# A new order of all engines from 45 microseconds on, in an attention and maxout kernel on one core

## The chip, the core and the metric

The kernel runs on one core of a Trainium2 chip. The metric is the time of one execution on the device, in microseconds, as the median of several runs. The engines of the core are TensorE (PE in the profile; its weight loads are PEld), VectorE (DVE), ScalarE (ACT), GpSimd (POOL) and SyncE (SP), which here issues nearly all transfers.

## What is computed

Attention over queries that are averaged in pairs, 8 batches of 8 heads with 1152 keys and 64 values each, and behind it a layer with two hidden projections of which the larger is taken:

```python
q_pool = q.reshape(B, H, S // 2, 2, D).mean(axis=3)        # B, H, S, D = 8, 8, 1152, 64
scores = scale * np.matmul(q_pool, k.transpose(0, 1, 3, 2))
attn = np.exp(scores - scores.max(-1)); attn = attn / attn.sum(-1)
x = np.matmul(attn, v)                                     # to (8 * 576, 512)
g = np.maximum(x @ w1, x @ w2)                             # w1, w2: 512 x 1024
return g @ w_out                                           # w_out: 1024 x 512
```

The kernel uses that max(a, b) = max(a − b, 0) + b: with wd = w1 − w2 and w21 = w2 w_out, the result is relu(x wd) w_out + x w21.

## The kernel before

Two heads that stand side by side are a *pair*; there are 32 pairs, four to a batch. For each pair SyncE loads q, k and v (576 KB each, lines 346, 358, 370) into rings of three buffers. GpSimd casts them to bfloat16: k at L405, v at L445, and q at L435, where the two rows of a query are also added. k is turned by a DMA transpose from SyncE (L475, `kT`), q on VectorE by eight 32 x 32 block transposes (L485, `qpT`), from pair 5 on.

The scores of all pairs are one stream of 324 *groups* of 512 columns (`scores`, L302). The two heads of a pair use the upper and lower 64 rows of the array at once, so a group is two rows' worth of matmuls with 64 contraction rows. One exp on ScalarE (L317) empties a group from two banks of PSUM into `et`. Attention (`av_jobs`) multiplies the exps by v with 128 contraction rows (L621), and the leftover 64 queries of a pair by blocks of 64 columns (L636). VectorE takes the reciprocal of the sums and multiplies (L651, L654) into `xnat`. The result is turned by a DMA transpose (L703, `xT`) or on TensorE (L552, L730, evacuated at L733, L738).

The second layer has *hidden-layer jobs* (h, L760), which make relu(x wd) for two blocks of 128 features over up to 512 tokens, and *projection jobs* (p, L803), which make 256 rows of the result. Both use 64-row halves: a first half-job runs every contraction block with the halves one way round, a second half-job the other way round into the same two banks. At the second half-job's start the plan puts a fence, a wait of TensorE for the end of the first:

```python
                    return ([f"wd{ct}.{half}" for half in range(2)] + xkeys(ct, n0, n1),
                            0.2135 * size / 512 + 0.0025, "s", turn == 1 and ct == 0, go)
```

h jobs are evacuated at L771 (VectorE) or L775 (ScalarE), p jobs at L809 or L812. At the end three jobs for the last 256 rows use the whole array (L846).

No scheduler runs on the chip. The order is written out by hand as tables that a search made: `LOADS` is the order of the loads on SyncE, `MOE` the order of the h, p and w jobs, `BANKS` the PSUM bank of each job and score group, and a long string of letters (L957 on) the order of all steps, one letter each. `S` is a group of scores, `E` its exp, `A` a block of attention, `a` its evacuation, `l` the next load, `r` one of the eight transposes of q, `t` a DMA transpose of k, `x` one of a result, and the digits 0 to 3 are one unit of the h or p job open in that slot, 4 to 7 its evacuation on VectorE, `8`, `9`, `+` and `-` the same on ScalarE. Each engine executes its own steps in the order of the string, and waits by semaphores for what a step reads or overwrites. From group 40 on a load also waits for the exp two groups back (`pace`):

```python
        def pace():
            g = done[0] - PACE
            return [f"E{g}"] if PACE and g >= PACE_FROM else []
```

Of the kernel before, what the change touches and what calls it, by code (L numbers as in the profile page):

```python
# [116 lines left out]
def bass_funnel_attn__then__act_maxout2_kernel(  # L117
# [39 lines left out]
    W_DIFFS = ((3, 0), (3, 1), (1, 0), (2, 0), (2, 1), (0, 0), (0, 1), (1, 1))  # L157
# [24 lines left out]
    )  # L182
    MOE = (
        "wwhhhhpphhhhpphhhhhhhhpphhhhpphhhhphhhhpphhhhphhhhphhhhpphhhhhhhhhphphh"
    )
    BANKS = (
        "0124605424023623462032424660232342630240624702402064202420472042646264246024604640164604264126402406"
        "0240260240246304260346204040640606062061262062062402740264062402406402640642704260202402402406401640"
        "6460462056204620462046042164206204620620426026402602602602604604614646046046024604604204620420642040"
        "6406406742064264264206520640260462620620162062046206240620206204230642042042424126426046046045620642"  # L190
        "6024062046206206206206412640246056046206404024024026423236042642042626260262626426454526420642064206"
        "2454"
# [849 lines left out]
```

## Time and profile before

| | us |
|---|---|
| median of 3 runs | 358.24 |
| the runs | 357.92, 358.24, 360.69 |
| the profiled execution's own time | 358.12 |
| its span, first to last instruction | 356.4 |
| TensorE busy | 346.0 |
| ScalarE busy | 313.8 |
| VectorE busy | 230.1 |
| GpSimd busy | 151.4 |

The time of an execution is 1.7 us longer than its span. In the profile a line such as "L760 PE MATMUL ps<-xT,wd" names the source line, the engine, the operation and what it writes and reads. A matmul's duration includes its way through the array, so the pace of matmuls is read from their starts. TensorE's clock was granted in full: 0.999 of it over the span.

### The profile page before, as it was taken

To read this page: it belongs to the slowest core of one execution; us is meant where nothing else is said; L and a number is where in the kernel's file an instruction comes from. 1 tells how busy PE (TensorE), PEld (TensorE's weight loads), DVE (VectorE), ACT (ScalarE), POOL (GpSimd) and SP (SyncE) were. 2 spreads that over 40 slices of the span, in tenths; PEclk is the share of its full clock that TensorE was granted. 3 is DMA by queue.
4 is the path that set the end of the run, shared out by engine and by line. 5 is a ranking of instruction groups with operands and counts; after the bars stand their busy time and mean duration, and the time that the engine had idled before them with its cause. 6 is when DMAs were issued, how large, how long until landed. Compare 5 with 4: busy or idle time off the path is not lost.

```text
span 356.4 us, 13757 instructions
## 1 busy us (share of the span) xinstructions
PE 346.0 (97%) x6178; PEld 218.5 (61%) x6178; DVE 230.1 (65%) x472; ACT 313.8 (88%) x354; POOL 151.4 (42%) x136
## 2 busy tenths in 40 slices
PE   7889999999899999999999999999999999999996
PEld 5556665656564675656666576556576757448753
DVE  2587589974966867985887677785586875414001
ACT  5999999999999899999999989989999796992431
POOL 2625997554564264355544455227444621010000
PEclk9999999999999999999999999999999999999999
DMA  8999999999989989998999699998999943012215
GB/s 271 403 397 398 370 255 309 280 289 261 293 252 279 315 196 350 237 301 183 278 320 260 153 230 301 237 314 234 224 299 255 267 68 75 17 32 47 61 31 148
DMA packets 76699, 84.55 MB, mean 237 GB/s; under 512 B 48480, under 2 KB 49760, under 8 KB 76640
## 3 DMA queue, kind: packets, MB, share of 16 engines
q1 hardware_dynamic: 75856, 83.15, 87.5%
q8 instruction: 48, 0.79, 0.9%
q10 hardware_dynamic: 784, 0.52, 0.5%
q14 instruction: 11, 0.09, 0.1%
HBM read 62.91 MB, written 9.44 MB: 203 GB/s over the span
## 4 chain that ended last, share of the span: by engine, by line
PE 87%; ACT 9%; DMA 2%; issue 1%; SPq 0%; DVE 0%
PE ps L803 25%; PE ps L621 20%; PE ps L302 19%; PE ps L760 16%; ACT et L317 9%; PE ps L636 3%; PE ps L593 2%; DMA qraw<-in_q_dram 2%; PE ps L846 1%; PE ps L552 0%; PE ps L533 0%; SPq L346 0%; DVE qp L428 0%; SPq L358 0%; PE ps L730 0%
## 5 line engine op out<-in xcount | busy, mean ns | idle before, releaser
L317 ACT ACTIVATE et<-ps 128x1024 bf16<-128x1024 f32 (+1 forms) x336 | 302.4, 1019 | 14.5 <-PE ps L302 9.7
L302 PE MATMUL ps<-qpT,kT 64*128 64x256 bf16 (+7 forms) x1162 | 117.3, 283 | 2.7 <-issue 1.1
L485 DVE STREAM_TRANSPOSE qpT<-qp 32x288 bf16<-32x288 bf16 x216 | 101.4, 469 | 10.4 <-PE ps L302 6.1
L760 PE MATMUL ps<-xT,wd 64*128 64x512 bf16 (+3 forms) x832 | 81.2, 311 | 0.2
L302 PEld LDWEIGHTS ps<-qpT,kT 64*128 64x128 bf16 x1162 | 48.3, 94 | 49.7 <-ACT et L317 11.3
L803 PE MATMUL ps<-wo,stage 64*128 64x512 bf16 x544 | 76.4, 376 | 0.0
L435 POOL TENSOR_TENSOR qp<-qraw 128x576 bf16<-128x576 f32 x30 | 42.1, 1406 | 61.1 <-DMA qraw<-in_q_dram 57.3
L621 PEld LDWEIGHTS ps<-vE,et 128*128 128x128 bf16 x1728 | 54.9, 97 | 13.9 <-ACT et L317 9.3
L621 PE MATMUL ps<-vE,et 128*128 128x65 bf16 x1728 | 60.7, 193 | 0.7 <-issue 0.3
L771 DVE TENSOR_SCALAR stage<-ps 128x1024 bf16<-128x1024 f32 (+3 forms) x41 | 39.7, 970 | 21.1 <-PE ps L760 20.6
L760 PEld LDWEIGHTS ps<-xT,wd 64*128 64x128 bf16 x832 | 35.6, 94 | 22.2 <-PE ps L760 1.9
L405 POOL TENSOR_SCALAR kbf<-kraw 128x1152 bf16<-128x1152 f32 x31 | 35.7, 1153 | 26.3 <-DMA kraw<-in_k_dram 25.6
L803 PE MATMUL ps<-w,xT 64*128 64x512 bf16 x272 | 40.8, 377 | 0.0
L803 PEld LDWEIGHTS ps<-wo,stage 64*128 64x128 bf16 x544 | 26.4, 94 | 20.5
L445 POOL TENSOR_SCALAR vE<-vraw 128x1152 bf16<-128x1152 f32 x24 | 27.4, 1154 | 19.4 <-PE ps L636 10.8
L809 DVE COPY stage<-ps 128x1024 f32<-128x1024 f32 x14 | 17.1, 1224 | 23.1 <-PE ps L803 23.0
L468 POOL TENSOR_SCALAR stage<-et 128x1152 bf16<-128x1152 bf16 x14 | 16.1, 1152 | 35.5 <-ACT et L317 35.5
L654 DVE TENSOR_TENSOR xnat<-ps,rc 128x256 bf16<-128x256 f32 (+2 forms) x71 | 27.6, 397 | 2.0
L651 DVE RECIPROCAL rc<-ps 128x4 f32<-128x4 f32 (+2 forms) x64 | 11.6, 182 | 25.9 <-PE ps L621 25.5
L621 PEld LDWEIGHTS ps<-stage,et 128*128 128x128 bf16 x576 | 18.1, 97 | 2.7 <-issue 2.6
L621 PE MATMUL ps<-stage,et 128*128 128x65 bf16 x576 | 19.7, 193 | 0.0
L803 PEld LDWEIGHTS ps<-w,xT 64*128 64x128 bf16 x272 | 12.5, 94 | 8.8 <-DVE stage L771 0.2
(55 smaller groups left out, 155.4 us busy)
## 6 DMA issues: line engine op xcount, KB each, us to landing
vraw<-in_v_dram SPq DMA_DIRECT2D x32, 576.0 KB, 6.1
kraw<-in_k_dram SPq DMA_DIRECT2D x31, 576.0 KB, 6.7
qraw<-in_q_dram SPq DMA_DIRECT2D x31, 576.0 KB, 6.3
out_dram<-stage SPq DMA_DIRECT2D x24, 256.0 KB, 4.1
out_dram<-stage SPq DMA_DIRECT2D x21, 128.0 KB, 3.4
xT<-in_moe_w_dram SPq DMA_DIRECT2D x4, 512.0 KB, 12.2
stage<-in_moe_w_out_dram SPq DMA_DIRECT2D x4, 512.0 KB, 14.1
stage<-in_moe_w_dram SPq DMA_DIRECT2D x4, 512.0 KB, 13.2
```

The source lines that it names most:

```text
L302: last = e.matmul(ps[:, h, col:col + hi - lo], kT[i % 3][rows(h), t, :], qpT[i % 3][rows(h), lo:hi], start=True, stop=True)
L317: op("ACT", lambda e: e.activation(et2[:, :, c:c + z - a], ps[:, :, a - g * W:z - g * W], EXP, scale=scale), r=[f"b{m}", f"b{m + 1}"], w=w ...
L405: op("POOL", lambda g: g.tensor_scalar(kbf[s][:, :, :, :].rearrange("p t h d -> p h t d"), kraw[r][:, :, :, :], 1.0, 1.0, ALU.mult, ALU.mu ...
L435: op("POOL", lambda g: g.tensor_tensor(qpf[s][:, :, :], qraw[r][:, :, 0, :], qraw[r][:, :, 1, :], ALU.add), r=[f"qraw{r}"], w=[f"qp{s}.0", ...
L445: return g.tensor_scalar(vE[r][:, :, :, 0:D].rearrange("p t h d -> p h t d"), vraw[s][:, :, :, :], 1.0, 1.0, ALU.mult, ALU.mult)
L485: op("DVE", lambda e: e.transpose(view[dst:dst + 32, :, 32 * pb:32 * pb + 32], qpf[s][src:src + 32, :, 32 * db:32 * db + 32]), r=[f"qp{s}. ...
L621: last = e.matmul(fb[m][:, at * 66:at * 66 + 65], et[:, a:a + P], vE[vs][:, t, half, 0:65], start=(t == 0), stop=(t == NT - 1))
L654: todo.append(evac_op("DVE", lambda e, m, z=z, at=at, num=num, dst=dst: e.tensor_tensor(dst, a(m)[z, at:at + num, 0:D], rc[k][z, at:at + n ...
L760: last = e.matmul(fb[m + k][:, 0:size], wd[z, ct, (f0 + k) * P:(f0 + k + 1) * P], xT[z, ct, n0:n1], start=(turn == 0 and ct == 0), stop=(t ...
L771: return e.tensor_scalar_max(gT[:, f0:f0 + 2, g0:g0 + size], wide[m // 2][:, :, 0:size], 0.0)
L803: last = e.matmul(fb[m + k][:, :], lhs, rhs, start=(turn == 0 and j == 0), stop=(turn == 1 and j == NC_ + NF - 1))
L809: return e.tensor_copy(osb2[:, o:o + 2, :], wide[m // 2][:, :, :])
```

## The change

Only the tables change: one place of `W_DIFFS` (two of the subtractions w1 − w2 swapped), the tail of `LOADS`, one line of `MOE`, `BANKS`, and the string of steps. Up to about 45 us each engine's order is as before. The h and p jobs now rotate through the four slots 0 to 3, where before they used two, and up to four are open at a time. The numbers and shapes of all instructions stay, but for the evacuations: 10 on ScalarE where it was 14 (without the last one, L854), and four more on VectorE. The diff, cut:

```diff
-    W_DIFFS = ((3, 0), (3, 1), (1, 0), (2, 0), (2, 1), (0, 0), (0, 1), (1, 1))
+    W_DIFFS = ((3, 0), (3, 1), (1, 0), (2, 0), (0, 0), (2, 1), (0, 1), (1, 1))
...
-        ("v", 12), ("q", 13), ("v", 13), ("k", 15), ("q", 14), ("v", 14), ("k", 16), ("v", 15),
...
+        ("q", 13), ("q", 14), ("k", 15), ("k", 16), ("v", 12), ("v", 13), ("v", 14), ("q", 15),
...
-        "wwhhhhpphhhhpphhhhhhhhpphhhhpphhhhphhhhpphhhhphhhhphhhhpphhhhhhhhhphhh"
+        "wwhhhhpphhhhpphhhhhhhhpphhhhpphhhphhhhhpphhhhphhhhphhhhpphhhhhhhphhhhp"
...
-        "6024062046206206206206412640246056046206404024024026423236042642042626260262626426454526420642064206"
-        "2454"
+        "6024063046216206206216402640240656046026404024024026431026402642042626260262626426454766240640246220"
+        "6565"
...
```

What this does to the engines' lists is shown at three places. Names carry buffer numbers there: `ps1` is the second of the four double banks of PSUM, `qpT2` the third buffer of turned queries, `xnat1` the odd batches' attention results.

TensorE at about 131 us, three hidden-layer jobs of 128 tokens (L760, two matmuls to a contraction block, eight to a half-job) among the scores (L302). Before:

```order
L760 MATMUL ps1<-xT,wd 128x128 x6
L302 MATMUL ps0<-qpT1,kT1 128x384 x2
L302 MATMUL ps0<-qpT1,kT1 128x128 x2
L760 MATMUL ps1<-xT,wd 128x128 x10
L760 MATMUL ps2<-xT,wd 128x128 x14
L302 MATMUL ps3<-qpT1,kT1 128x448 x2
L302 MATMUL ps3<-qpT1,kT1 128x64 x2
L760 MATMUL ps2<-xT,wd 128x128 x2
L760 MATMUL ps1<-xT,wd 128x128 x10
L302 MATMUL ps0<-qpT1,kT1 128x512 x2
L760 MATMUL ps1<-xT,wd 128x128 x6
```

The same place now:

```order
L760 MATMUL ps1<-xT,wd 128x128 x8
L302 MATMUL ps0<-qpT1,kT1 128x384 x2
L302 MATMUL ps0<-qpT1,kT1 128x128 x2
L760 MATMUL ps1<-xT,wd 128x128 x8
L760 MATMUL ps2<-xT,wd 128x128 x8
L302 MATMUL ps3<-qpT1,kT1 128x448 x2
L302 MATMUL ps3<-qpT1,kT1 128x64 x2
L760 MATMUL ps1<-xT,wd 128x128 x6
L760 MATMUL ps2<-xT,wd 128x128 x8
L760 MATMUL ps1<-xT,wd 128x128 x10
```

Before, the second half of each of the three jobs follows its first half directly, inside the rows x10, x14 and x10. Now scores or another job's matmuls stand between in the first two, and only the last row x10 goes straight from the first half into the second.

VectorE ahead of the first scores of pair 20 (group 202, 197.4 us in the profile of before); `qpT2<-qp0` are the eight transposes of that pair's q. Before:

```order
L771 TENSOR_SCALAR stage<-ps1 128x2x384
L485 STREAM_TRANSPOSE qpT2<-qp0 32x9x32 x2
L771 TENSOR_SCALAR stage<-ps3 128x2x384
L485 STREAM_TRANSPOSE qpT2<-qp0 32x9x32
L651 RECIPROCAL rc0<-ps0 128x4
L654 TENSOR_TENSOR xnat0<-ps0,rc0 128x4x64
L485 STREAM_TRANSPOSE qpT2<-qp0 32x9x32 x3
L771 TENSOR_SCALAR stage<-ps3 128x2x384
L485 STREAM_TRANSPOSE qpT2<-qp0 32x9x32
L651 RECIPROCAL rc1<-ps1 128x4
L654 TENSOR_TENSOR xnat0<-ps1,rc1 128x4x64
L485 STREAM_TRANSPOSE qpT2<-qp0 32x9x32
```

And now:

```order
L771 TENSOR_SCALAR stage<-ps3 128x2x384
L485 STREAM_TRANSPOSE qpT2<-qp0 32x9x32 x7
L809 COPY stage<-ps1 128x1024
L651 RECIPROCAL rc0<-ps3 128x4
L654 TENSOR_TENSOR xnat0<-ps3,rc0 128x4x64
L651 RECIPROCAL rc1<-ps3 128x4
L654 TENSOR_TENSOR xnat0<-ps3,rc1 128x4x64
L485 STREAM_TRANSPOSE qpT2<-qp0 32x9x32
```

The eighth transpose stood ahead of the last of the four h evacuations (`128x2x384`); now it stands behind them, behind a projection's evacuation (L809) and behind both halves of the attention of pair 18.

SyncE at 140 to 175 us, the DMA transposes of the results of pairs 12, 13 and 14 (`xT<-xnat1`) among loads and the transposes of k. Before:

```order
L703 DMA_TRANSPOSE xT<-xnat1 128x4x128
L370 DMA vraw2<-in_v_dram 128x2x576
L358 DMA qraw0<-in_q_dram 128x1152
L346 DMA kraw0<-in_k_dram 128x2x576
L703 DMA_TRANSPOSE xT<-xnat1 128x4x128
L475 DMA_TRANSPOSE kT2<-kbf1 128x9x128
L370 DMA vraw0<-in_v_dram 128x2x576
L358 DMA qraw1<-in_q_dram 128x1152
L346 DMA kraw1<-in_k_dram 128x2x576
L475 DMA_TRANSPOSE kT0<-kbf0 128x9x128
L703 DMA_TRANSPOSE xT<-xnat1 128x4x128
```

And now:

```order
L475 DMA_TRANSPOSE kT0<-kbf0 128x9x128
L370 DMA vraw2<-in_v_dram 128x2x576
L358 DMA qraw1<-in_q_dram 128x1152
L358 DMA qraw2<-in_q_dram 128x1152
L703 DMA_TRANSPOSE xT<-xnat1 128x4x128 x3
L835 DMA out_0_dram<-stage 64x512 x3
L370 DMA vraw0<-in_v_dram 128x2x576
```

The three transposes of results moved behind the loads and the transposes of k and stand together.

More of the change, by code (lines that the diff above doesn't have):

```diff
@@ new lines, in bass_funnel_attn__then__act_maxout2_kernel @@
+            "SrEAdaAaSEltaaAaAdAaEASaXaEdXjSjEjXSqjSElj222qEr2SSr22Elr23kr33Er32St63lE3S3v3E7S00E00vSrS0Er00er0SE"
+            "l4AAAElSSAEAaAaAEArSrESEAeaaAAEAAqaSrSElaAAAkESa1r11Eak1tSr22Er22Sr2E1r1Sr11Ell25S22E22SSE22332E2e2S"
+            "2Elt22Sq22E2S22Elv2S633E3S33Elr33rSSE3rArAAErSrAElxArArSvAEaxAaSa3aE3kSrS3r3ESkr333rE33rqS3Elr33r33E"
+            "S7AAElxASSEAtvAAEASaSaElAaAAaEAASaSaEaSrXErAAjAElAjSa0a0ESr0v0rSEl0r00r0qEltS1r11rE1S4e11E11S5SEAAAE"
+            "ASa2aE22Er2eSrSE222v2SE6AAAvElloSSoAEkAoaAaAEAkSa3aE3Sr00qr0E0rS33rElt0Sr33Er33S70E0t0S00ErSe0r0SE0r"
@@ new lines, in bass_funnel_attn__then__act_maxout2_kernel @@
+            "00r0ESrS0r0E0r00k0rElo00S41qE11S11Eo1SSol1E1111qESAtAEAAAaAaAA1EaSak1E1rS222r211ErS2222r11Elo1rxS161"
+            "E1SSx1E1A5AEAxlllkASrSESrArAAEAaAaAlEAaAaSa3333aESa333370000ES222000vl02E42222S6XEjSv1jo11rE1oSr1o1E"
+            "rv1tl1rSS5EAeAAlEArqSSrElAArArEA3aSa3E3a3aS3rE3eESrS3r3EA7AAEASa0rE0Sqa00rSE0r000rEllStrAAE4qSAAESa2"
+            "ka2E22SSE2t222SE6AAAEASa1aE11rkSSr1E1r11e1rESSr11Ellvr11rS1Er111rq1E1r1SrSE1rtllAArEAASa1aE11S13E533"
+            "S3E3SrS3r3E33r3SEAAvAEAS3vElxSAAEAxAaSa3ESaxAaArAEArSo3aE3aoSa3oll3XEeSj33j3E3roSqSr3E3r33SEk7AAAEAS"
@@ L987, in bass_funnel_attn__then__act_maxout2_kernel @@
+            "EAAAEAAaAaAeAAaEAaAAxAaAaAAtSaSaE1111oSE0o111oE1So500Exll0S00E002433S3oE33rS2r2E2Sr22Er22rS36E3S333E"
+            "S331E1eS33E3Sv33E3S33vE33S3E317S11E1S1o1E1So11Eo1SoS1E1AAEAAAaAaAAAaAaAxAAAAAaAaAAaAa1a1a1a11X1j11j1"
+            "100009233330000222343332221o-111000o0331111335000203+333812722211122200020+0000000033331222211123933"
+            "322720+000001322223023220002213122203102422111232o222o22o2233+1Z5ZZZ-ZoZZoZZZZZZZmZZZZzzZZZZZZZZZZmZ"
             "ZZZZZZzZzmzz"
```

50 lines of the change are left out of this document (18 added, 32 removed), and 16 rows, old and new, of the table LOADS.

## Prediction

> **What bounds the kernel now.** I read the page first, then the chain of waits in order of time, the busy time by stretches, and who waited for whom. The page:
>
> ```profile
> span 356.4 us, 13757 instructions
> ...
> PE 346.0 (97%) x6178; PEld 218.5 (61%) x6178; DVE 230.1 (65%) x472; ACT 313.8 (88%) x354; POOL 151.4 (42%) x136
> ...
> PE 87%; ACT 9%; DMA 2%; issue 1%; SPq 0%; DVE 0%
> ```
>
> TensorE is busy for 97% of the span, ScalarE for 88%, and the chain that ended last is TensorE's for 87%. A busy TensorE may still hide short stalls, since matmul ends are modelled, so I ask where the chain leaves it. From 45 us on these pieces of the chain in order of time are all that last over a microsecond and are not TensorE's:
>
> ```profile
> 44.70 13.43 ACT et L317 x15
> 58.14 1.95 ACT et L317 x2
> ...
> 91.57 1.12 issue
> ...
> 181.62 1.95 ACT et L317 x2
> ```
>
> So the searched part has two regimes: up to 60.1 us the exps (L317) set the pace, after that TensorE's own list of instructions does, with a wait of 1.12 us at 91.57 that no semaphore explains and a short return to the exps at 181.62. The stretches say how much time TensorE leaves (columns: length, then busy time and count of PE, PEld, DVE, ACT, POOL):
>
> ```profile
> 45.00:60.00 15.00, 14.59 (x250) 8.08 (x246) 13.08 (x28) 14.99 (x18) 13.72 (x12) 1.00 1.16 283
> 60.00:135.00 75.00, 73.54 (x1362) 46.86 (x1364) 56.08 (x121) 72.94 (x83) 37.49 (x32) 1.00 1.02 272
> 135.00:210.00 75.00, 74.94 (x1364) 47.52 (x1362) 56.23 (x119) 73.23 (x82) 36.03 (x30) 1.00 1.06 254
> 210.00:285.00 75.00, 74.99 (x1371) 48.26 (x1366) 55.74 (x117) 69.88 (x79) 35.42 (x30) 1.00 1.07 268
> ```
>
> Visible idle time of PE between 45 and 285 us is 0.41 + 1.46 + 0.06 + 0.01 = 1.94 us. That, and what stalls hide inside "busy", is all that a better order can win, because the order changes no matmul: both kernels have 6178, in the same shapes.
>
> **What TensorE waits for inside its busy time.** From the view of waits (microseconds in total, times, longest):
>
> ```profile
> PEld ps L302 <- ACT et L317: 11.3, 48, 0.5
> ...
> PEld ps L621 <- ACT et L317: 9.3, 27, 0.6
> ...
> PEld ps L760 <- PE ps L760: 1.9, 7, 0.3
> ...
> PE ps L302 <- issue: 1.1, 1, 1.1
> ```
>
> The first two are weight loads that wait while earlier matmuls still run; they cost little, as the stretches show. The third is the one that a row of the timeline turns into lost time. A hidden-layer job runs four pairs of row halves, then four pairs the other way round into the same banks, and the second half begins behind a wait for the first:
>
> ```profile
> 130.86 0.33 PE L760 MATMUL ps<-xT,wd 64*128 64x128 bf16 x6
> 131.03 0.38 PE L302 MATMUL ps<-qpT,kT 64*128 64x384 bf16 x4
> 131.24 1.32 PE L760 MATMUL ps<-xT,wd 64*128 64x128 bf16 x24
> 132.40 0.38 PE L302 MATMUL ps<-qpT,kT 64*128 64x448 bf16 x4
> 132.61 0.74 PE L760 MATMUL ps<-xT,wd 64*128 64x128 bf16 x12
> 133.19 0.38 PE L302 MATMUL ps<-qpT,kT 64*128 64x512 bf16 x2
> ```
>
> Six matmuls (three pairs) take 131.03 − 130.86 = 0.17 us, 0.057 a pair. Then 24 (12 pairs) take 1.16 us where 0.68 would do, and 12 (6 pairs) 0.58 where 0.34 would: 0.48 + 0.24 = 0.72 us, three stalls of 0.24, one for each of the three jobs whose second half follows its first directly.
>
> **Part by part.**
>
> *The hidden-layer jobs at 131 us (PE rows in the section on the change).* Before, the rows x10, x14 and x10 each run from the end of a first half into the second half of the same job. Now two of these three jobs have other matmuls there; only the last x10 (three pairs of it come earlier, as x6) still runs through. Two stalls go: −2 × 0.24 = −0.48 us, in a stretch where the chain is TensorE's, so all of it counts. Bounds: 0 (the exps are late there instead) to −0.48.
>
> *One change of tile shape less.* At 46 us two blocks of 18 matmuls (L636) that had scores between them now stand together: one trip from 64-row tiles to 128-row tiles and back less, of 86 such trips in all. Its price, from this row group and the next fence: 36 attention matmuls take 61.33 − 60.13 = 1.20 us, 72 take 196.09 − 193.81 = 2.28, so 36 more cost 1.08 and a trip's one side is 1.20 − 1.08 = 0.12; the scores' side is 61.87 − 61.33 = 0.54 against 196.53 − 196.09 = 0.44 for as many columns, 0.10.
>
> ```profile
> 60.13 1.26 PE L621 MATMUL ps<-vE,et 128*128 128x65 bf16 x36 [0.25 <-ACT et L317]
> 61.33 0.61 PE L302 MATMUL ps<-qpT,kT 64*128 64x320 bf16 x8
> 61.87 0.51 PE L621 MATMUL ps<-vE,et 128*128 128x65 bf16 x11
> ```
>
> It is worth 0.22 us, but lies in the exps' stretch of 44.70 to 58.13, where TensorE's spare time goes into waiting: I take 0, bounds 0 and −0.22. [...]
>
> *The q transposes (L485, eight for each pair of heads, VectorE).* Scores of a pair need all eight. In the list of steps the last of them stood a median of 13 score groups ahead of its first user; now the median is 3, and for 10 of 27 pairs (8, 11, 13, 14, 18, 19, 20, 22, 24, 31) it is 1 or 2. VectorE works in order, so each now stands behind whatever precedes it. For pair 20 that is the reciprocal and product of the attention just finished. In the trace of before the same spot is:
>
> ```profile
> 193.81 2.35 PE L621 MATMUL ps<-vE,et 128*128 128x65 bf16 x72
> ...
> 196.09 0.61 PE L302 MATMUL ps<-qpT,kT 64*128 64x128 bf16 x8
> 196.19 0.18 DVE L651 RECIPROCAL rc<-ps 128x4 f32<-128x4 f32 x1 [0.45 <-PE ps L621]
> ...
> 196.41 0.42 DVE L654 TENSOR_TENSOR xnat<-ps,rc 128x256 bf16<-128x256 f32 x1
> ...
> 196.53 1.03 PE L803 MATMUL ps<-w,xT 64*128 64x512 bf16 x8
> ...
> 197.40 0.60 PE L302 MATMUL ps<-qpT,kT 64*128 64x256 bf16 x8
> ...
> 197.82 0.47 DVE L485 STREAM_TRANSPOSE qpT<-qp 32x288 bf16<-32x288 bf16 x1 [0.99 <-PE ps L302]
> ```
>
> The row at 197.40 begins with pair 20's first scores. TensorE's work between the attention and these scores is the same as before, only divided otherwise (a group of scores and four projection matmuls, twice), so they still fall due 1.31 us after the attention. VectorE would end the product at 196.83 and, if the transpose follows, that at 197.33: 0.07 us ahead of need. It just fits. For the ten places together I take +0.3 us. Bounds: below by 0, since no row shows TensorE waiting for these transposes today and nothing can be won there; above by one more product or transpose (0.42 to 0.47) missing at each, 10 × 0.45 = 4.5 us.
>
> *Loads and DMA transposes (SyncE).* Three transposes of attention results (pairs 12 to 14, L703) used to be spread out and now stand together behind a load of q. That load waits for the exp of score group 166 (loads stay two exps behind), the second in this row, and the hidden-layer job that reads the results is at 174.65:
>
> ```profile
> 162.41 1.96 ACT L317 ACTIVATE et<-ps 128x1024 bf16<-128x1024 f32 x2
> ...
> 174.65 0.65 PE L760 MATMUL ps<-xT,wd 64*128 64x384 bf16 x6
> ...
> L703 SPq DMA_TRANSPOSE xT<-xnat x24: 1188/1236/1891, 64.0 to 323.4; - x24
> ...
> DMA to landing us min/median/max: 2.5/4.4/7.1
> ```
>
> Exp over at 164.37; the load 0.4; three issues of 1.24; the third issues at about 167.3 and lands between 169.8 and 174.4, by min and max of the last row. The job needs the third result as its third pair, about 175.0. It is hidden, with 0.6 us to spare at the worst landing. I take 0; bounds 0 and +2 (three queued together that take half as long again). The loads themselves are as many and as large; v is fetched later, and as TensorE waits for no load from 45 us on, they are put at 0.
>
> *Evacuations.* Four evacuations in the last 30 us go from ScalarE to VectorE (one other goes the other way in the stretch 210 to 285, where ACT has 75.00 − 69.88 = 5.1 us free): 0.
>
> Sum on the profiled execution: 358.12 (span 356.4 and 1.7 around it) − 0.48 + 0 + 0.3 = 357.94. That execution is 0.12 under the median of the runs shown, 358.24. Forecast 358.1 us.
>
> **The rivals.**
>
> *Just-in-time transposes miss (slower).* Everything above holds, but VectorE runs a little behind the order's own plan, and at each of the ten places TensorE stands until the transpose lands. For it: the spare time is 0.07 us at pair 20, where 197.82 in the row before shows transposes that also wait for TensorE. Against it: the row at 196.19 shows VectorE idle just ahead, so it begins as soon as the attention ends. Missing by one operation each gives 358.1 − 0.3 + 4.5 = 362.3 us; it decides from 0.36 us a place, which makes 3.6 us, the 1% that I count as different from no change.
>
> *The bundled DMA transposes land late.* The third at 175.0 + 1 to 2 us, and the same at other bundles (pairs 8 to 10, 21 to 23): against it stands the worst landing of 7.1 us, which fits. About +1.5 us: 359.6.
>
> *The waits of before go as well (faster).* If the new order also fills the 0.41 us before 60 us, avoids the 1.12 at 91.57 and pays nothing for the transposes, it is 358.1 − 0.3 − 1.5 = 356.3. Against it: the exps' stretch is 14.99 of 15 busy on ACT, and the wait at 91.57 has no releaser that an order could move. More than 3.6 us cannot be reached: 1.94 of idle time, 0.48 and 0.22 make 2.64.
>
> *The edit does nothing:* the stalls at 131 us come back as a wait for the exps. 358.1 + 0.48 = 358.6; this is inside the forecast's own range.
>
> **How the numbers follow.** Forecast 0.62 (its own range 357.0 to 359.2), late transposes of q 0.14, late DMA transposes 0.12, fewer waits 0.12. Left out below the low end is half of the last (0.06), above the high end most of the first rival (0.10). Range 356.0 to 361.2. Faster by over 1% (under 354.7) 0.03 for what the trace doesn't show, slower (over 361.8) 0.14, within 1% 0.83.
>
> **What would show it.** Right: one stall in place of three in the rows of L760 with 64x128 near 131 us; waits of L302 for L485 in the list of PE or PEld that sum to well under a microsecond; a chain that stays on PE after 60 us. Wrong: a row "ps L302 <- DVE qpT L485" of several microseconds (first rival), "ps L760" or "ps L302" waiting for a DMA of xT or kT (second), or the exps' part of the chain longer than 9%.

## The result and the profile after

| | before | after |
|---|---|---|
| median of 10 runs (lowest, highest) | 358.41 (356.96, 360.69) us | 360.75 (358.62, 362.40) us |
| ratio, 95% interval | | 1.0053 [1.0033, 1.0072] |
| profiled execution, its span | 358.12, 356.4 us | 362.40, 360.4 us |

The new order is about half a per cent slower, inside the forecast's range but on the other side of the kernel before. Three executions in this document, one of e1 and two of the kernel before, were over 1.5% above the fastest of their kernel and are left out of the ratios and of the counts of executions. The profiled execution is the longest of the ten, so its losses are larger than usual; a second profile of the same kernel (first experiment) has a span of 357.1 us. The page of the changed kernel (busy time, then the shares of the chain that ended last):

```profile
span 360.4 us, 13722 instructions
...
PE 350.6 (97%) x6177; PEld 221.6 (61%) x6178; DVE 233.0 (65%) x476; ACT 312.5 (87%) x350; POOL 150.9 (42%) x136
...
PE 87%; ACT 8%; DMA 2%; DVE 1%; issue 1%; POOL 0%
```

The same matmuls (one record of the 6178 is missing), and the chain has nearly the same shares: no engine became a new bound. I therefore compared when each score group starts in the two traces. Group 40, at 44 us, starts 1.04 us later in after, a difference of the start, where each engine's order is the same; from 71 to 88 us it is 0.99 us. Then the new order loses in two places: the difference is 3.42 us at 109 us and 3.95 at 147 us, and 4.03 at the last groups.

**At 92 us.** TensorE's rows of the timeline, first of before, then of after (start, duration, operation, count, idle time ahead and what ended it):

```profile
91.18 0.39 PE L302 MATMUL ps<-qpT,kT 64*128 64x64 bf16 x4
92.70 0.61 PE L302 MATMUL ps<-qpT,kT 64*128 64x128 bf16 x8 [1.12 <-issue]
...
93.46 1.26 PE L621 MATMUL ps<-vE,et 128*128 128x65 bf16 x36
```

```profile
92.17 0.39 PE L302 MATMUL ps<-qpT,kT 64*128 64x64 bf16 x3
93.89 0.65 PE L302 MATMUL ps<-qpT,kT 64*128 64x448 bf16 x8 [1.33 <-issue]
...
95.36 1.98 PE L621 MATMUL ps<-vE,et 128*128 128x65 bf16 x36 [0.54 <-ACT et L317]
```

Both pause without a releaser. The first row is group 91 of the scores, two matmuls of 64 columns and two of 448. Before, all four ran ahead of the pause (x4); after, three did (x3), and the fourth, on which the exp of group 91 waits, came behind it. The next attention (L621) reads that exp and writes a bank which it empties, in both orders. So after has a second wait straight behind the first. A third loss follows. Busy time by stretches (length; busy time and count of PE, PEld, DVE, ACT, POOL; granted clock; share of the DMA engines; GB/s):

```profile
92.20:95.60 3.40, 1.52 (x34) 1.09 (x33) 2.21 (x7) 1.71 (x3) 0.00 (x0) 1.00 0.77 218
95.60:99.00 3.40, 3.40 (x48) 2.49 (x46) 1.54 (x4) 2.55 (x3) 2.18 (x2) 0.50 0.82 235
99.00:105.00 6.00, 6.00 (x90) 3.31 (x88) 4.76 (x8) 5.72 (x7) 1.46 (x2) 1.00 0.99 210
```

TensorE was busy for 1.52 of 3.40 us, and in the next 3.4 us its clock was granted at 0.50. So half clock followed a stretch of 3.4 us that was busy for 45%. In e15 it followed one of 53% (1.80 of 3.40 us; 0.55 over the next 3.4 us); in e9 and e2, after stretches of 53% and 51%, it didn't come (1.000 over the span of both), so no share of busy time that brings it can be read off. Not every execution shows this: the mean granted clock was 0.995 in 4 of the 10 runs of after.

**At 135 to 148 us.** The chain of waits in order of time leaves TensorE for a load:

```profile
134.54 0.64 ACT et L317
135.18 8.48 DMA qraw<-in_q_dram
143.74 1.41 POOL qp L435
145.17 0.47 DVE qpT L485
145.65 0.47 DVE qpT L485
146.14 0.47 DVE qpT L485
146.60 1.12 DVE stage L771
147.77 0.61 PE ps L760 x4
```

The q of pair 15 lands at 143.66, GpSimd adds its rows, three of its transposes hold VectorE, the evacuation of a hidden-layer job stands behind them, and TensorE waits. By the starts of the matmuls around it that wait is 0.50 us.

**At the fences.** The rows that answer to those of 131 us:

```profile
134.78 0.68 PE L760 MATMUL ps<-xT,wd 64*128 64x128 bf16 x16
135.62 0.39 PE L302 MATMUL ps<-qpT,kT 64*128 64x448 bf16 x4 [0.16 <-ACT et L317]
135.84 1.07 PE L760 MATMUL ps<-xT,wd 64*128 64x128 bf16 x24
136.75 0.38 PE L302 MATMUL ps<-qpT,kT 64*128 64x512 bf16 x2
...
137.45 0.39 PE L302 MATMUL ps<-qpT,kT 64*128 64x512 bf16 x2
```

Only the row x24 keeps a fence stall (0.91 us from 135.84 to 136.75, where 12 pairs at 0.057 would take 0.68). But the scores at 135.62 and 137.45 now wait for the exps.

In what follows, a pause or a wait is measured by the starts of matmuls: the gap to the next one, less its pace.

### The profile page after: what moved, and what is told of

It is laid out like the page before. It is cut to its first block, busy times and chain, and to the rows that moved or that the text cites. A ratio compares the mean times of both kernels' runs of the same rounds, so it can differ in the third digit from the quotient of the medians.

```text
span 360.4 us, 13722 instructions
## 1 busy us (share of the span) xinstructions
PE 350.6 (97%) x6177; PEld 221.6 (61%) x6178; DVE 233.0 (65%) x476; ACT 312.5 (87%) x350; POOL 150.9 (42%) x136
## 4 chain that ended last, share of the span: by engine, by line
PE 87%; ACT 8%; DMA 2%; DVE 1%; issue 1%; POOL 0%
PE ps L803 25%; PE ps L302 19%; PE ps L621 19%; PE ps L760 15%; ACT et L317 8%; PE ps L636 3%; DMA qraw<-in_q_dram 2%; PE ps L593 2%; PE ps L515 2%; PE ps L846 1%; PE ps L552 1%; PE ps L533 0%; POOL qp L435 0%; DVE qpT L485 0%; DVE stage L771 0%
## 5 line engine op out<-in xcount | busy, mean ns | idle before, releaser
L317 ACT ACTIVATE et<-ps 128x1024 bf16<-128x1024 f32 (+1 forms) x336 | 303.5, 1018 | 16.6 <-PE ps L302 12.4
L302 PE MATMUL ps<-qpT,kT 64*128 64x256 bf16 (+7 forms) x1162 | 115.0, 287 | 2.8 <-issue 1.3
L760 PE MATMUL ps<-xT,wd 64*128 64x512 bf16 (+3 forms) x832 | 78.7, 312 | 0.7 <-DVE stage L771 0.3
L302 PEld LDWEIGHTS ps<-qpT,kT 64*128 64x128 bf16 x1162 | 48.8, 95 | 49.2 <-ACT et L317 8.7
L803 PE MATMUL ps<-wo,stage 64*128 64x512 bf16 x544 | 72.6, 376 | 0.0
L621 PEld LDWEIGHTS ps<-vE,et 128*128 128x128 bf16 x1728 | 55.6, 97 | 12.6 <-ACT et L317 8.1
L771 DVE TENSOR_SCALAR stage<-ps 128x1024 bf16<-128x1024 f32 (+3 forms) x44 | 41.0, 933 | 34.3 <-PE ps L760 33.9
L621 PE MATMUL ps<-vE,et 128*128 128x65 bf16 x1728 | 61.5, 194 | 0.7 <-ACT et L317 0.5
L760 PEld LDWEIGHTS ps<-xT,wd 64*128 64x128 bf16 x832 | 35.6, 94 | 23.1 <-ACT et L317 1.1
L803 PE MATMUL ps<-w,xT 64*128 64x512 bf16 x272 | 38.5, 376 | 0.0
L468 POOL TENSOR_SCALAR stage<-et 128x1152 bf16<-128x1152 bf16 x14 | 16.1, 1151 | 47.9 <-ACT et L317 47.9
L809 DVE COPY stage<-ps 128x1024 f32<-128x1024 f32 x15 | 18.3, 1221 | 24.6 <-PE ps L803 24.5
L651 DVE RECIPROCAL rc<-ps 128x4 f32<-128x4 f32 (+2 forms) x64 | 11.8, 184 | 34.1 <-PE ps L621 33.6
L654 DVE TENSOR_TENSOR xnat<-ps,rc 128x256 bf16<-128x256 f32 (+2 forms) x71 | 27.6, 397 | 2.0
L621 PEld LDWEIGHTS ps<-stage,et 128*128 128x128 bf16 x576 | 18.1, 97 | 3.0 <-issue 2.6
L621 PE MATMUL ps<-stage,et 128*128 128x65 bf16 x576 | 19.7, 193 | 0.0
```

The source lines that it names most:

```text
L302: last = e.matmul(ps[:, h, col:col + hi - lo], kT[i % 3][rows(h), t, :], qpT[i % 3][rows(h), lo:hi], start=True, stop=True)
L317: op("ACT", lambda e: e.activation(et2[:, :, c:c + z - a], ps[:, :, a - g * W:z - g * W], EXP, scale=scale), r=[f"b{m}", f"b{m + 1}"], w=w ...
L621: last = e.matmul(fb[m][:, at * 66:at * 66 + 65], et[:, a:a + P], vE[vs][:, t, half, 0:65], start=(t == 0), stop=(t == NT - 1))
L654: todo.append(evac_op("DVE", lambda e, m, z=z, at=at, num=num, dst=dst: e.tensor_tensor(dst, a(m)[z, at:at + num, 0:D], rc[k][z, at:at + n ...
L760: last = e.matmul(fb[m + k][:, 0:size], wd[z, ct, (f0 + k) * P:(f0 + k + 1) * P], xT[z, ct, n0:n1], start=(turn == 0 and ct == 0), stop=(t ...
L771: return e.tensor_scalar_max(gT[:, f0:f0 + 2, g0:g0 + size], wide[m // 2][:, :, 0:size], 0.0)
```

## The experiments

Every run gives its median (of 10 to 12 executions; seven in e9, four in e7) beside that of the kernel before on the same chip. The first ten rows are the changed kernel with the edit named, the others start from the kernel before or join edits. "92 us" is the pause without a releaser there, "exp" the wait of attention for the exp behind it, "140s" the longest wait of TensorE for VectorE between 141 and 153 us, each in the one profile taken.

| run | edit | median | before | ratio, 95% interval | 92 us | exp | 140s |
|---|---|---|---|---|---|---|---|
| e1 | none | 360.07 | 359.07 | 1.0031 [1.0001, 1.0061] | 1.05 | 0.61 | 0.30 |
| e2 | 56 instructions more at the start | 359.64 | 359.07 | 1.0016 [0.9991, 1.0041] | 0 | 0.23 | 1.17 |
| e4 | q 15 loaded ahead of v 12 to 14 | 361.78 | 359.07 | 1.0062 [1.0032, 1.0091] | 1.49 | 0.61 | 1.19 |
| e5 | 2 instructions fewer at the start | 358.20 | 359.01 | 1.0000 [0.9976, 1.0023] | 0.67 | 0 | 0 |
| e18 | the same again | 358.61 | 358.30 | 0.9999 [0.9971, 1.0028] | 0 | 0.23 | 0.82 |
| e7 | q 15 and k 16 exchanged | 361.67 | 359.01 | 1.0091 [1.0058, 1.0125] | 1.05 | 0.61 | 0 |
| e9 | 3 transposes behind L771 | 360.17 | 358.81 | 1.0060 [1.0035, 1.0085] | 1.22 | 0.61 | 1.23 |
| e15 | 3 transposes behind L771 and L654 | 360.63 | 358.15 | 1.0083 [1.0050, 1.0116] | 1.22 | 0.61 | 0.87 |
| e11 | three transfers before 92 us later | 358.10 | 358.81 | 1.0007 [0.9986, 1.0029] | 0 | 0.22 | 1.49 |
| e12 | q 15 one place earlier | 359.85 | 358.99 | 1.0025 [0.9999, 1.0051] | 0 | 0.23 | 0 |
| e10 | e5 and e9 | 359.31 | 358.81 | 1.0014 [0.9991, 1.0038] | 0 | 0.22 | 1.23 |
| e13 | e11 and e12 | 358.80 | 358.99 | 1.0004 [0.9980, 1.0027] | 0 | 0.23 | 1.19 |
| e16 | e11 and e15 | 359.00 | 358.15 | 1.0021 [1.0004, 1.0039] | 0.04 | 0.44 | 0.88 |
| e17 | e5 and e12 | 358.19 | 358.30 | 0.9986 [0.9957, 1.0015] | 0 | 0.23 | 0.53 |
| e3 | before, 56 instructions more | 359.38 | 359.07 | 1.0000 [0.9975, 1.0025] | 0.62 | 0.23 | 0 |
| e6 | before, 2 instructions more | 359.61 | 359.01 | 1.0031 [1.0006, 1.0056] | 1.46 | 0.61 | 0 |
| e8 | before, no second half behind its first | 359.02 | 359.01 | 0.9990 [0.9961, 1.0019] | 0.99 | 0 | 0.31 |
| e14 | before, v 9 four groups later | 359.01 | 358.99 | 1.0007 [0.9985, 1.0028] | 1.00 | 0 | 0.05 |

**e1 to e3: the kernel again, and TensorE's stream shifted.** In e2 and e3 56 warming matmuls (`FILL`; nothing reads what they write) of half the width stand where 28 stood, as many columns in all, with 56 instructions more (a weight load and a matmul each):

```diff
-    FILL = 28
+    FILL = 56
...
-                op("PE", lambda e: fill(e, 7, FILL), r=["rem0"], w=["b7"], cost=0.0563 * FILL, mode="f",
+                op("PE", lambda e: fill(e, 7, FILL, 64), r=["rem0"], w=["b7"], cost=0.0563 * FILL, mode="f",
```

> The changed kernel unchanged, to see every run's granted clock beside its time. [...]

> The same order, but the idle matmuls at the very start are 56 of 64 columns instead of 28 of 128, so that 56 more instructions of TensorE stand ahead of everything else. Theory A1 (the stall at 92 us is TensorE running out of fetched instructions, at a fixed place in its list counted in instructions, the 3265th matmul or weight load): the stall keeps the count 3265 and so comes 56 instructions earlier in the program, among other matmuls, or goes away if the fetch is then in time; the time falls by 1 to 2 us where the clock stays whole. Rival A2 (something in the program at group 91 is waited for): the stall stays at group 91, count 3321.

> The same 56 short matmuls in the kernel before. Theory A1: its stall of 1.29 us moves to the same count or goes, and the time changes by at most 1.3 us. Rival A2: stall at the same scores, no change of time.

The unchanged kernel shows the pause again ahead of the same matmul, with the same 0.61 us behind it, so its place belongs to the program and not to one execution. Shifted, the pause of before moves forward into the attention (0.62 us at 91.48), by exactly the 28 matmuls that were added at the start; that of after is gone from 92 us. e2 came out at half of e1's loss, but its interval and e1's overlap widely. That the instruction count matters is seen; what it costs is not.

**e4: q of pair 15 ahead of three loads of v.**

```diff
-        ("q", 13), ("q", 14), ("k", 15), ("k", 16), ("v", 12), ("v", 13), ("v", 14), ("q", 15),
+        ("q", 13), ("q", 14), ("k", 15), ("k", 16), ("q", 15), ("v", 12), ("v", 13), ("v", 14),
```

> The new order with one load moved: q of pair 15 ahead of v of pairs 12, 13 and 14, which the new order loads in one burst. Theory C (the 0.50 us wait of TensorE at 147.8 us comes from this burst: q lands late, its cast and its transposes on VectorE come late, and a hidden-layer evacuation stands behind them): that wait goes, 0.3 to 0.5 us less. Rival D (the evacuation is late for another reason, such as the attention ahead of it): the wait stays, no change.

A miss: q 15 landed at 135.15 instead of 143.66, but GpSimd casts in its own order, so q 15's step still stood behind the casts of the now later v and ended at 145.07. The wait for L771 grew to 1.19, and attention waited 0.47 for v. The table leaves out a fourth loss: at 144.2 us scores waited 1.20 us for an exp (L317) that itself waited for a copy on GpSimd (L468) behind the same casts. What has to be early is the cast, not the load alone.

**e5, e6 and e18: the pause moved by one weight load and one matmul.** If the pause falls at a fixed count of instructions, one warming matmul fewer puts it behind the last matmul of group 91 in after, and one more puts it ahead of that matmul in before:

```diff
-    FILL = 28
+    FILL = 27
```

```diff
-    FILL = 28
+    FILL = 29
```

> The changed kernel with 27 instead of 28 warming matmuls at the start, so that each later instruction of TensorE stands two places (a weight load and a matmul) earlier in its stream. Theory A: the pause without a releaser at 92 us falls at a fixed count of instructions. In the changed kernel it falls just ahead of the last matmul of score group 91, so the exp of 91 and the attention that needs its bank come late; in the kernel before it falls just behind that matmul. Here the pause stays (1.0 to 1.5 us), but lies behind the last matmul of group 91; the wait of attention (L621) for an exp, 0.54 us in the page of the changed kernel, goes, and with it the half clock that some runs had: median 359.0 to 359.7 us, 0.6 to 1.1 below the changed kernel's. Rival: the new order itself leaves too little lead of the exps there; the wait of 0.5 stays, and the time is the changed kernel's, 360.1 to 360.8 us.

> The kernel before with 29 instead of 28 warming matmuls, so that each later instruction of TensorE stands two places later in its stream. Theory A: the pause at 92 us moves ahead of the last matmul of score group 91, and the kernel before gets the wait that the changed one has: 0.5 to 0.6 us of L621 for an exp straight behind the pause, and half clock for one stretch in some runs; median 0.5 to 1.1 us above the kernel before. Rival: the place of the pause doesn't matter, and its time is the kernel before's within 0.2 us.

TensorE's timeline of the changed kernel with 27:

```profile
90.90 0.39 PE L302 MATMUL ps<-qpT,kT 64*128 64x64 bf16 x4
91.80 0.61 PE L302 MATMUL ps<-qpT,kT 64*128 64x128 bf16 x8 [0.51 <-issue]
...
92.56 1.26 PE L621 MATMUL ps<-vE,et 128*128 128x65 bf16 x36
```

and of the kernel before with 29:

```profile
90.62 0.39 PE L302 MATMUL ps<-qpT,kT 64*128 64x64 bf16 x3
92.30 0.65 PE L302 MATMUL ps<-qpT,kT 64*128 64x448 bf16 x8 [1.29 <-issue]
...
93.76 1.26 PE L621 MATMUL ps<-vE,et 128*128 128x65 bf16 x36 [0.54 <-ACT et L317]
```

x4 and x3 have changed sides, and with them the wait for the exp. The times follow: the changed kernel falls to the time of before, further than expected, and before rises by the ratio that e1 had. The cleaner test is e6, whose pause is as long as that of after (1.46 us); in e5 the pause itself is shorter than expected (0.67), so its gain isn't that of the place alone.

Why the new order has the pause one matmul earlier can be counted. These are TensorE's instructions until the pause ends, first those that only wait (L99), then matmuls (first count) and weight loads (second count); before, then after:

```profile
L99 PEldq EVENT_SEMAPHORE  x22: 51/51/51, 2.6 to 78.1; - x22
0.00:92.69 92.69, 85.74 (x1620) 54.09 (x1621) 64.53 (x129) 87.65 (x98) 53.98 (x56) 1.00 1.03 325
```

```profile
L99 PEldq EVENT_SEMAPHORE  x24: 51/51/98, 2.6 to 91.6; - x24
0.00:93.88 93.88, 88.69 (x1619) 55.37 (x1620) 62.48 (x125) 86.79 (x97) 52.58 (x54) 1.00 1.02 304
```

Both make 3263 (3265 with two at the program's start), and so do the other ten profiles with the pause, whether 27, 28, 29 or 56 of the matmuls are warming ones. The new order has two more waits there, at 82.26 and 91.55 us: groups 81 and 91, the first scores of pairs 8 and 9, wait for more than one thing now (the exp, the DMA transpose of k, at 81 also VectorE's transposes of q), and a further wait takes an instruction of its own. So it isn't only the evacuations whose number changed, as the section on the change has it; and the 27 of e5 take out two instructions, as many as the new waits add.

> The changed kernel with 27 warming matmuls a second time, to see beside the run above what q 15 early adds. As the first time: at the kernel before within 0.4 us, no wait of L621 for an exp at 94 us. If q 15 is late in this execution, a wait of 0.3 to 1.2 us for L771 stands at 141 to 148 us; the first time there was none. Rival: the first result was luck of the chip, and the time is the changed kernel's, 1 us or more above the kernel before.

The repeat agrees (0.9999). Of the four profiles with 27 (e5, e10, e17, e18) three have no pause at all, against one of seven with the 28 of after and its transfers (e12); why isn't settled. Without the pause two short waits stand there, 0.24 us for the product L654 and 0.23 for the exp: 0.5 us together, against a pause of 1.0 to 1.3 in before (before, e8, e14). So with 27 the kernel gains some 0.5 us more than the place is worth, and its equality with before doesn't say that nothing is lost elsewhere.

**e11 and e14: fewer transfers ahead of the pause.** `l` (here the loads of q 11, then v 9) and `t` (k 10) stand later; in e14 one `l`, the load of v 9:

```diff
-            "S7AAElxASSEAtvAAEASaSaElAaAAaEAASaSaEaSrXErAAjAElAjSa0a0ESr0v0rSEl0r00r0qEltS1r11rE1S4e11E11S5SEAAAE"
+            "S7AAExASSEAvAAEASaSaElAaAAaEAASaSaEaltSrXErAAjAElAjSa0a0ESr0v0rSEl0r00r0qEltS1r11rE1S4e11E11S5SEAAAE"
```

> The changed kernel with the loads of q 11 and v 9 and the DMA transpose of k 10 issued four to six score groups later, so that about 1.2 MB less is queued on the DMA engines in the 5 us ahead of the pause at 92 us. Theory F: the pause is a fetch of instructions that is late behind other transfers; it shrinks below 0.6 us (0.5 to 1.5 us in the profiles so far). Rival: the pause doesn't depend on the transfers, and stays between 0.9 and 1.5 us.

> The kernel before with the load of v 9 issued four score groups later (576 KB less queued ahead of the pause at 92 us). Theory F: the pause (1.29 and 0.99 us in two profiles of this order) is a late fetch of instructions behind other transfers, in the kernel before as well; it shrinks below 0.6 us or goes, and the time falls by 0.4 to 1.0 us. Rival: one load less isn't enough, or the pause belongs to that place: it stays at 0.9 to 1.5 us and the time doesn't change.

In e11 the scores run through where the pause was, but the wait in the 140s takes much of it back (timeline of TensorE):

```profile
90.39 0.87 PE L302 MATMUL ps<-qpT,kT 64*128 64x64 bf16 x12
...
144.06 0.60 PE L760 MATMUL ps<-xT,wd 64*128 64x512 bf16 x4 [1.33 <-DVE stage L771]
```

All three profiles with these transfers later (e11, e13, e16) are without the pause (0.04 us at most), and one of their 34 runs had the clock at 0.995. The page of after has a queue of instructions, whose packets are of 16 KB (0.79 MB in 48):

```profile
q8 instruction: 48, 0.79, 0.9%
```

In every profile with the pause one of them lands 1.2 to 1.6 us before it ends (in after at 92.63, 1.26 us ahead of the row at 93.89); in six without it (e10 to e13, e17, e18) it landed 1.5 to 2.3 us before group 91 began, and in e16, with 0.04 us left, 1.1 us before. With the fixed count of instructions this makes a wait for a packet of instructions the best reading of the pause; no edit moved such a packet alone. That data transfers make it late is less sure: e11 speaks for it, but in e14 one load issued later left before's pause at 1.00 us, and in e12 it was missing without an edit to the transfers there.

**e7: q 15 and k 16 exchanged, loads and casts.**

```diff
-        ("q", 13), ("q", 14), ("k", 15), ("k", 16), ("v", 12), ("v", 13), ("v", 14), ("q", 15),
+        ("q", 13), ("q", 14), ("k", 15), ("q", 15), ("v", 12), ("v", 13), ("v", 14), ("k", 16),
```

> The changed kernel with the loads of q of pair 15 and k of pair 16, and their casts, exchanged: q 15 is then issued ahead of the three DMA transposes of results and the three loads of v that it stood behind. Theory C: q 15 lands at about 132 us instead of 143.7, its transposes are done long before the evacuation of the hidden-layer job (L771), and the wait of L760 for L771 at 144.5 to 147.8 us (0.30 and 0.50 us in the two profiles of the changed kernel) goes: time 0.3 to 0.5 us below the changed kernel. Rival: the evacuation is late by its own place behind TensorE, and the wait stays; or k of pair 16 comes late instead and L302 waits for kT near 160 us, more than 0.5 us.

The cast of q 15 now overwrites pair 13's buffer ahead of the last three transposes of pair 13, which read the queries of pair 15 here, so this version leaves out part of the queries of pair 13. VectorE waited for that cast, and TensorE 1.81 us for VectorE at 132.66. The wait for L771 was gone, but with 1.81 and 1.28 us of new waits ahead of it this tells nothing of the theory.

**e9, e10 and e15: q 15 late as it is, other steps first.** Three transposes of pair 15 behind L771 (e9, and with 27 in e10); three behind L771, L651 and L654 as well, where a fourth stood already, and one left ahead (e15, its new line below):

```diff
-            "rv1tl1rSS5EAeAAlEArqSSrElAArArEA3aSa3E3a3aS3rE3eESrS3r3EA7AAEASa0rE0Sqa00rSE0r000rEllStrAAE4qSAAESa2"
+            "rv1tl1rSS5EAeAAlEArqSSrElAArArEA3aSa3E3a3aS3E3eESS33EA7rrrAAEASa0rE0Sqa00rSE0r000rEllStrAAE4qSAAESa2"
```

```diff
+            "rv1tl1rSS5EAeAAlEArqSSrElAArArEA3aSa3E3a3aS3rE3eESS33EA7AAEASa0E0Sqa00rrrrSE0r000rEllStrAAE4qSAAESa2"
```

> The changed kernel with three of the eight q transposes of pair 15 moved on VectorE from ahead of the evacuation of a hidden-layer job (L771) to straight behind it; loads as in the changed kernel. Theory C: q of pair 15 lands late, its first transposes hold VectorE, and the evacuation and TensorE stand behind them; with the transposes behind the evacuation the wait of L760 for L771 at 144 to 148 us (0.30 and 0.50 us in two profiles) is gone however late q lands, and no wait of L302 for L485 takes its place, as the scores of pair 15 come 8 us later: 0.3 to 0.5 us off, 359.6 to 360.4 us beside the changed kernel's 360.07 to 360.75. Rival: the evacuation is late for TensorE's own half-job or for the bank, and a wait of 0.3 us or more stays there.

> Both small edits in the changed kernel: 27 warming matmuls, and the three q transposes of pair 15 behind the evacuation. If the pause's place and the late load are the two costs of the new order, both waits are gone from the profile and this is the fastest of the kernels run: 357.9 to 358.6 us median, 0.3 to 1.0 us below the kernel before. Rival: the order has other costs that these two hid; then it is at the kernel before, within 0.2 us, or above it.

> The changed kernel with four of the eight q transposes of pair 15 moved on VectorE behind the hidden-layer evacuation (L771) and behind the reciprocal and product of the attention that follows it (L651, L654); loads and casts as in the changed kernel. Theory C3: the load of q 15 is late by what is queued ahead of it, and costs only through the VectorE steps that stand behind its transposes. With all steps that TensorE waits for ahead of them, no wait over 0.2 us stands at 144 to 148 us; the pause at 92 us and its 0.6 us of ACT stay: 0.3 to 0.9 us under the changed kernel (360.1 to 360.8 so far). Rival: the transfers bound this stretch whatever stands on VectorE, and a wait of 0.5 us or more comes up at the scores of pair 15 (L302 for L485) or at a cast of v instead.

All three missed. The wait moved each time and didn't go: 1.23 us for the product L654 in e9 and e10, 0.87 for the next evacuation in e15. VectorE in e15, and the row of TensorE that waits for it:

```profile
144.91 0.47 DVE L485 STREAM_TRANSPOSE qpT<-qp 32x288 bf16<-32x288 bf16 x1 [0.89 <-POOL qp L435]
...
147.59 3.37 DVE L485 STREAM_TRANSPOSE qpT<-qp 32x288 bf16<-32x288 bf16 x7
150.99 1.22 DVE L771 TENSOR_SCALAR stage<-ps 128x1024 bf16<-128x1024 f32 x1
```

```profile
152.27 1.04 PE L760 MATMUL ps<-xT,wd 64*128 64x512 bf16 x8 [0.71 <-DVE stage L771]
```

From 144.91 to 152 VectorE has no gap but 0.35 us: the eight transposes (3.84 us) must fit between the cast of q 15 and its scores, beside the evacuations. Whatever stands behind them is late when the cast is late.

**e12, e13, e16 and e17: q 15 earlier, and edits joined.** In e12 the load of k 16 goes behind q 15, and its cast too:

```diff
-        ("q", 13), ("q", 14), ("k", 15), ("k", 16), ("v", 12), ("v", 13), ("v", 14), ("q", 15),
+        ("q", 13), ("q", 14), ("k", 15), ("v", 12), ("v", 13), ("v", 14), ("q", 15), ("k", 16),
```

> The changed kernel with the load of k 16 moved from ahead of the DMA transposes of results to behind q 15, so that v 12, v 13, v 14 and q 15 are each issued one place earlier (v 12 ahead of the three transposes); the cast of k 16 follows that of q 15. Theory C2: q 15 landing late behind what SyncE and the DMA engines have queued is what stops TensorE at 144 to 148 us, by whichever VectorE step stands behind its transposes: the evacuation L771 in the changed kernel (0.30, 0.50, 1.49 us in three profiles), the product L654 where the transposes were put behind that (1.23). With q 15 landing 2 to 5 us earlier, before the hidden-layer job ends, both waits are gone: under 0.1 us there; the pause at 92 us stays as it is; time 0.4 to 1.0 us under the changed kernel's on the same chip (360.1 to 360.8 so far). Rival: the transfers of results (L703) now land too late, and L760 waits near 135 us.

> Both: fewer transfers ahead of the pause at 92 us (as in the run with three issues later there) and q 15 early. If the late instruction fetch and the late q are the two costs of the new order, no wait over 0.35 us is left after 60 us, and this is the fastest of all: 357.0 to 357.8 us median, 0.8 to 1.5 us below the kernel before on the same chip. Rival: other costs remain, and it is within 0.4 us of the kernel before.

> The same edit together with the three later issues ahead of 92 us. With only the later issues the pause went, but a wait of 1.49 us for L771 at 144 us took the gain back. Theory C3: now neither is there, and nothing over 0.35 us is left after 60 us: 356.8 to 357.8 us median, 0.9 to 1.6 us under the kernel before on the same chip. Rival: the transfers give the gain back at another place, and it is within 0.4 us of the kernel before.

> The changed kernel with the two edits that each took one wait out at its cause: 27 warming matmuls (the pause at 92 us falls behind the last matmul of group 91), and k 16 loaded behind q 15. If the place of the pause and the late q 15 are the loss, the time is at or under the kernel before on the same chip: 357.3 to 358.5 us median, 0.3 to 1.0 us below it, and neither a wait of L621 for an exp at 94 us nor one of L760 for L771 over 0.3 us at 141 to 148 us is in the profile. Rival: more is lost elsewhere, and it stays above the kernel before.

e12 lost both waits in its profile (span 355.7 us), but other executions seem to have had the pause: 3 of its 12 runs had the clock at 0.994 or 0.995, and the median is 359.85. In e13 q 15 was late again: the three DMA transposes of results ahead of it held SyncE for 8.63 us, and at 142.4 us scores waited 1.07 us for an exp behind L468, as in e4. SyncE's queue in e13, then in after:

```profile
124.06 8.63 SPq L703 DMA_TRANSPOSE xT<-xnat  x3
132.74 1.10 SPq L370 DMA_DIRECT2D vraw<-in_v_dram  x2
133.88 0.47 SPq L358 DMA_DIRECT2D qraw<-in_q_dram  x1
```

```profile
127.81 5.01 SPq L703 DMA_TRANSPOSE xT<-xnat  x3
132.86 2.28 SPq L370 DMA_DIRECT2D vraw<-in_v_dram  x3
135.18 0.47 SPq L358 DMA_DIRECT2D qraw<-in_q_dram  x1
```

Over the profiles of after and of edits that leave VectorE's order alone, the wait follows how long after the first score of group 140 the cast of q 15 ends: 2.22 us (e12) and 2.77 (e5) no wait, 3.33 (e1) 0.30, 3.52 (after) 0.50, 3.56 (e17) 0.53, 3.84 (e18) 0.82, 4.20 (e2) 1.17, 4.51 (e11) 1.49. In e4 (5.57) and e13 (5.45) it is 1.19 in both, but there TensorE had already stood 1.20 and 1.07 us for the exp in between. In the orders of before the cast ends between 0.22 us ahead of that score and 0.56 behind it, and the largest such wait is 0.31. When TensorE gains time at 92 us, the transfers don't come earlier by as much (the 4.51 us of e11 and 3.84 of e18 against 3.33 and 3.52 in e1 and after), so part of the gain is given back here. e13 and e16, which each should have been the fastest, weren't; their profiles show waits of 1.19 and 0.88 us here. e17 has the lowest ratio of all, 0.9986 [0.9957, 1.0015], though q 15 was late there too (0.53, where at most 0.3 was expected); no version was shown to beat the kernel before.

**e8: the fences alone, in before.** Units of the next job or a score group now stand between the halves of the three jobs at 131 us:

```diff
-            "1rE0l001rS141E1rS1r1ES5AAEvAAroSSrvoESAlAAEvAaAaAlEAaAkaSa000SaEt0a000011114Ee111S111115E1S111Xl5EvS"
+            "1rE0l001rS141E1rS1r1ES5AAEvAAroSSrvoESAlAAEvAaAaAlEAaAkaSa000SaEt0a111100004Ee111S111115ES1111Xl5EvS"
```

> The kernel before with the second halves of the three hidden-layer jobs at 131 us no longer straight behind their first halves (other units, or a score group, stand between). The prediction's step: the three stalls of 0.24 us go and all of it counts, 0.48 to 0.72 us less than the kernel before. Rival: the exps set the pace at this place; the stalls go from the rows of L760, and waits of L302 or L621 for the exp (L317) of together 0.3 to 0.7 us stand in their place; time within 0.2 us of the kernel before.

TensorE's rows there:

```profile
131.65 1.15 PE L760 MATMUL ps<-xT,wd 64*128 64x128 bf16 x24
132.64 0.38 PE L302 MATMUL ps<-qpT,kT 64*128 64x448 bf16 x4
132.85 0.69 PE L760 MATMUL ps<-xT,wd 64*128 64x128 bf16 x10
...
134.38 0.39 PE L302 MATMUL ps<-qpT,kT 64*128 64x512 bf16 x2
```

From 131.26 to 134.38 the same work takes 3.12 us; in before the rows from 130.86 to 133.97 take 3.11. The three stalls of L760 for L760 are gone, and waits of 0.29 us for the product L654, 0.24 for the evacuation L771, and 0.08 and 0.24 for the exps stand in their place. The rival is right, though not only the exps take over. The rows decide this; the ratio's interval alone would leave room for 0.72 us. Between 140 and 146 us e8 also loses 0.7 us that before doesn't, which wasn't followed up.

## Why the prediction was wrong

The step that failed first is in the rival of the waits that go: "the wait at 91.57 has no releaser that an order could move". The wait has no releaser, but the order moved its place: it comes after a fixed count of TensorE's instructions, and the new order has two more waits ahead of it. I looked for what ended the wait, not for what it cut in two. One matmul of group 91 on the other side costs 0.61 us at once, and sometimes half clock: 17 of 63 executions of the versions with the 28 warming matmuls and the changed order's transfers before 92 us (after, e1, e4, e9, e12, e15; not e7, in whose profile, with a mean clock of 0.991, half clock stands at 134 us, behind other waits) had a granted clock of 0.996 or less, 2 of 48 with 27, and 11 of 160 of the kernel before. For before such executions are 1.5 us longer in the mean (360.13 against 358.61). So an estimated 0.61 + (17/63 − 11/160) × 1.5 = 0.91 us of the loss is here; e6 has 1.1 us by its ratio for the same shift in the kernel before.

The second is "as TensorE waits for no load from 45 us on, they are put at 0". Loads that nobody waits for have slack, and the new order used it up for q 15: GpSimd's cast ended 0.14 us ahead of the first score of group 140 and now ends 3.5 behind. That the three bundled DMA transposes hold SyncE (5.01 us in after) and what is queued there was priced for pairs 12 to 14 alone, as their own landing, and not for the loads behind pairs 8 to 10. Cost: 0.30 and 0.50 us in the two profiles of this order, up to 1.49 where TensorE comes earlier (e11). The link from the cast to the wait is read from the row of profiles; an edit that takes the late q away and keeps it away in every execution wasn't found.

The term of −0.48 for the fences was mis-sized. Two of three stalls went as forecast, but with the waits for exps, evacuation and product between 131 and 134.5 us in before (0.94 us together) and between 134.8 and 137.7 in after (0.84), 0.10 is left. Its own bound, 0, "the exps are late there instead", was nearly the value, and e8 shows it without the rest of the change.

The q transposes, +0.3, cost 0.05: in after the weight loads of L302 wait for them four times, and matmuls lose time at one of these, 113.84.

```profile
PEld ps L302 <- DVE qpT L485: 1.2, 4, 0.4
```

So the just-in-time rival didn't come; at pair 20 VectorE ended 0.08 us ahead of the scores (201.21 against 201.28). The landing of DMA transposes at 0 was right too: no matmul waits for a DMA of xT or kT. The place of one tile-shape trip less was put at 0; in the exps' stretch of 46 to 63 us the waits sum to 1.3 us before and 1.5 after. The 1.7 us around the span was carried over from before (1.74 in the mean); executions of after are 1.96 us longer than their spans, and every version of the changed order is above before there (1.83 to 2.15). That is 0.2 us more, whose cause stays open.

Of 0.91 + 0.4 (late q) + 0.15 (a wait for L771 at 99.8 us in e1) + 0.2 (exps) + 0.05 (q transposes) − 0.10 + 0.2 (outside the span) the sum is 1.8 us, between the 1.1 (e1) and 1.9 us (first ten runs) that the ratios give. That the time lay inside the range is luck: its upper part stood for transposes of q that miss their scores and DMA transposes that land late, and neither came.

## What to carry to other kernels

Price a wait without a releaser by what lies on both sides of it, and when an order or an instruction count changes, look which producer's last instruction falls behind it: moving one matmul across it cost 0.61 us in each such profile here, and about 1.1 us by the ratio of e6. Waits count as instructions too: two more of them moved the pause by one matmul here. "No engine waits for a load" is a statement about slack, so a change of the queue has to be followed load by load, through the cast and the engine behind it, with all that holds the queue ahead. And a stall that goes is a gain only up to the next one that was already due; undoing it alone in the old kernel (e8: three stalls of 0.24 us gone, 3.12 us in place of 3.11) measures that cheaply.

## What the runs showed of the hardware

The pause comes at a fixed place of TensorE's instruction stream: after 3263 matmuls, weight loads and separate waits in all twelve profiles that have it, so that two instructions more or fewer at the start moved it across one matmul more than 80 us later. TensorE's clock was granted at 0.50 for 3.4 us after a stretch of the same length that was busy for 45% (after), and at 0.55 after one of 53% (e15), but in full after stretches of 53% (e9) and 51% (e2). Three DMA transposes of 128 x 4 x 128 in a row held SyncE's queue for 5.0 us in after, and for 4.3 (e5) to 8.6 us (e13) in other profiles, while the kernel's order asked for much the same transfers around them.
